# First chunk of a convolution moved from VectorE to TensorE, input weights cast once and copied, output weights scaled on GpSimd

## The chip, the cores and the metric

The kernel runs on one core of a Trainium2 chip. The time is that of the device in microseconds (us), as the median of several executions. Engines are named as the profile names them: PE is TensorE (PEld its weight loads), DVE is VectorE, ACT is ScalarE, POOL is GpSimd, SP is SyncE.

## The reference, cut to what matters

```python
# x: 8 x 4096 x 192, weight: 8 heads x 7 taps; 24 neighbouring channels share a head
w = softmax(weight)                                          # over the 7 taps
x = sum(w[head, k] * x_padded[:, s + k, :] for k in 0..6)    # causal, along the sequence
h = x.reshape(32768, 192) @ w_in                             # w_in: 192 x 2048
g = h * sigmoid(beta * h)
out = g @ w_out                                              # w_out: 2048 x 192
```

A depthwise convolution of seven taps feeds two matrix products with an activation between them.

## The kernel before

The work goes in 33 stages. A full stage is a chunk of 512 positions from each half of the batch; the first chunk is split into stages 0 and 1, of 256 positions. In stage s PE computes the hidden layer of chunk s and, interleaved with it in 16 units, the output layer of stage s-1. ACT applies the activation. DVE convolves chunks ahead of time, one tap per instruction, and also evicts PE's finished outputs from PSUM, the memory that PE's sums go to (an eviction copies them out and frees the buffer).

```python
psum_h = tile_pool("psum_h", bufs=2, PSUM)   # hidden sums, 2 banks each
psum_o = tile_pool("psum_o", bufs=2, PSUM)   # output sums "po", 2 banks each: PSUM is then full

def conv_ops(s):                             # 21 taps of DVE for stage s
    def tap(j, k):
        ...
        if k == 0:
            nc.vector.tensor_scalar_mul(dst, src, scalar)
        else:
            nc.vector.scalar_tensor_tensor(out=dst, in0=src, scalar=scalar, in1=dst, op0=ALU.mult, op1=ALU.add)
    return [lambda j=j, k=k: tap(j, k) for j in range(NG) for k in range(K)]

def output(s, u):                            # PE's output sums, then DVE's eviction of them
    ...
            if fc == NF - 1 and b == 1:
                nc.vector.tensor_copy(dst, po[:, 0, 0 : 2 * D])
                nc.vector.tensor_tensor(dst, po[:, 1, 0 : 2 * D], dst, ALU.add)
    ...

for op in conv_ops(0):
    op()
queue = deque((1, op) for op in conv_ops(1))
for c in range(0, NF, 4):
    queue.append((1, lambda c=c: prep_w_out(c, 4)))     # w_out / beta, on DVE
...
for s in range(N_ST + 1):
    if s + 2 < N_ST:
        queue.extend((s + 2, op) for op in conv_ops(s + 2))
    for u in range(NF):
        hidden(s, u)                                    # if s < N_ST
        output(s - 1, u)                                # if s > 0
        for _ in range(2 - u % 2):                      # 24 taps may be emitted per stage
            if queue:
                queue.popleft()[1]()
        ...
```

Before these stages, the first chunk is loaded as fp32, transposed on PE, and convolved by 42 taps of DVE. All later chunks come through a cast in DRAM and a transposing transfer.

## Time and profile before

The median is 722.34 us (722.22 to 722.58, three runs). Two lines of the profile's page, busy times and the chain that ended last:

```profile
PE 682.1 (95%) x11379; PEld 521.8 (73%) x11379; DVE 601.6 (84%) x965; ACT 576.9 (80%) x535; POOL 63.6 (9%) x79
...
PE 91%; DVE 6%; DMA 2%; SPq 1%; issue 0%
```

PE is busy nearly all the time, and the chain is PE's. What can be saved lies where PE is not busy. The table of stretches shows where that is. Its columns are the stretch, its length, then for each engine busy us and number of instructions, the granted clock, and two DMA columns that are not used here.

```profile
0.00:22.00 22.00, 4.99 (x19) 3.68 (x19) 5.65 (x16) 3.90 (x7) 14.57 (x25) 1.00 1.03 175
22.00:28.80 6.80, 0.79 (x4) 0.24 (x5) 6.37 (x16) 0.00 (x0) 3.14 (x4) 1.00 2.23 174
28.80:40.00 11.20, 9.23 (x94) 5.72 (x95) 10.56 (x24) 9.82 (x16) 4.09 (x5) 1.00 1.79 157
40.00:50.50 10.50, 10.43 (x214) 9.98 (x215) 10.18 (x17) 10.12 (x16) 4.55 (x5) 1.00 2.17 141
50.50:58.60 8.10, 1.24 (x18) 0.65 (x14) 7.78 (x13) 1.03 (x2) 5.20 (x6) 0.75 2.31 167
58.60:79.30 20.70, 20.67 (x280) 13.98 (x281) 19.93 (x32) 18.86 (x19) 11.56 (x14) 0.93 2.19 165
```

The first number after the length is PE. It is nearly idle to 28.8 us, works through stages 0 and 1, is nearly idle again from 50.5 to 58.6, and is full from there on. What ended the idle times from 22 to 60 us is in the table of waits (us in total, times, longest):

```profile
PE ph L256 <- DVE ct L239: 12.6, 4, 4.6
PE ph L256 <- DMA xd<-in_x_dram: 4.5, 1, 4.5
PE ph L256 <- ACT g L263: 1.2, 5, 0.4
```

PE's hidden matmuls (`ph`) wait for DVE's taps (`ct`). DVE was busy with taps nearly without a gap, and two lines of its timeline in that stretch (start, duration) show what else it did:

```profile
39.12 3.56 DVE L216 TENSOR_TENSOR w_out_s<-w_out_raw,beta_r 128x768 bf16<-128x768 f32 x4
...
49.42 0.55 DVE L296 COPY osb<-po 128x384 f32<-128x384 f32 x1
```

The second line is an eviction.

### The profile page before, as it was taken

To read this page: it belongs to the slowest core of one execution; us is meant where nothing else is said; L and a number is where in the kernel's file an instruction comes from. 1 tells how busy PE (TensorE), PEld (TensorE's weight loads), DVE (VectorE), ACT (ScalarE), POOL (GpSimd) and SP (SyncE) were. 2 spreads that over 40 slices of the span, in tenths; PEclk is the share of its full clock that TensorE was granted. 3 is DMA by queue.
4 is the path that set the end of the run, shared out by engine and by line. 5 is a ranking of instruction groups with operands and counts; after the bars stand their busy time and mean duration, and the time that the engine had idled before them with its cause. 6 is when DMAs were issued, how large, how long until landed. Compare 5 with 4: busy or idle time off the path is not lost.

```text
span 719.3 us, 24695 instructions
## 1 busy us (share of the span) xinstructions
PE 682.1 (95%) x11379; PEld 521.8 (73%) x11379; DVE 601.6 (84%) x965; ACT 576.9 (80%) x535; POOL 63.6 (9%) x79
## 2 busy tenths in 40 slices
PE   2387999999999999999999999999999999999997
PEld 2264777777777777777777777777777777777776
DVE  1999999999999889898888989888898988887223
ACT  1386888888888888888888888888888888888881
POOL 7345553000000000000000000000000000000000
PEclk9998999999999999999999999999999999999999
DMA  9999999522222231222222123222212222211012
GB/s 158 184 148 166 168 175 168 79 63 68 68 59 58 69 67 35 60 68 68 47 69 69 37 55 68 69 46 68 69 43 50 68 68 47 69 46 46 25 46 69
DMA packets 189768, 55.77 MB, mean 78 GB/s; under 512 B 153296, under 2 KB 189664, under 8 KB 189664
## 3 DMA queue, kind: packets, MB, share of 16 engines
q0 software_dynamic: 100576, 14.11, 28.9%
q1 hardware_dynamic: 89040, 40.07, 24.1%
q8 instruction: 89, 1.46, 0.8%
q14 instruction: 15, 0.12, 0.1%
q10 hardware_dynamic: 48, 0.01, 0.0%
HBM read 30.58 MB, written 37.70 MB: 95 GB/s over the span
## 4 chain that ended last, share of the span: by engine, by line
PE 91%; DVE 6%; DMA 2%; SPq 1%; issue 0%
PE po L287 46%; PE ph L256 45%; DVE ct L239 4%; DMA x_83<-in_x_dram 2%; SPq L112 1%; DVE w_out_s L216 0%; DVE ct L237 0%; PE ph L201 0%; DVE osb L297 0%; DVE osb L296 0%; DVE xt L208 0%
## 5 line engine op out<-in xcount | busy, mean ns | idle before, releaser
L263 ACT ACTIVATE g<-ph,beta 128x1024 bf16<-128x1024 f32 (+1 forms) x528 | 573.0, 1090 | 112.0 <-PE ph L256 107.9
L239 DVE SCALAR_TENSOR_TENSOR ct<-xt,cw,ct 128x512 bf16<-128x512 bf16 (+1 forms) x594 | 436.1, 734 | 17.7
L256 PE MATMUL ph<-ct,w_in_s 64*128 64x512 bf16 (+1 forms) x3168 | 429.4, 372 | 19.0 <-DVE ct L239 12.6
L287 PEld LDWEIGHTS <-g 64*128 64x128 bf16 x8192 | 369.7, 94 | 102.7 <-issue 1.2
L287 PE MATMUL po<-w_out_s,g 64*128 64x192 bf16 x8192 | 430.3, 243 | 0.1
L256 PEld LDWEIGHTS <-w_in_s 64*128 64x128 bf16 x3168 | 164.3, 94 | 75.5 <-issue 18.2
L296 DVE COPY osb<-po 128x384 f32<-128x384 f32 x128 | 71.2, 556 | 75.2 <-PE po L287 74.9
L297 DVE TENSOR_TENSOR osb<-po,osb 128x384 f32<-128x384 f32 x128 | 71.4, 558 | 4.4
L94 POOL DMA_DIRECT2D xd<-in_x_dram x62 | 56.4, 909 | 54.3 <-DMA xd<-in_x_dram 49.8
L237 DVE TENSOR_SCALAR ct<-xt,cw 128x512 bf16<-128x512 bf16 (+1 forms) x99 | 35.3, 357 | 0.0
L201 PE MATMUL ph<-ident,x_83 128*128 128x128 f32 x12 | 3.5, 432 | 8.3 <-DMA x_83<-in_x_dram 8.3
L211 ACT CAST xt<-ph 128x256 bf16<-128x256 f32 x2 | 0.7, 373 | 12.8 <-DVE xt L208 12.8
L208 DVE CAST xt<-ph 128x512 bf16<-128x512 f32 x2 | 1.4, 692 | 10.5 <-PE ph L201 10.5
L201 PEld LDWEIGHTS ph<-ident,x_83 128*128 128x128 f32 x12 | 2.2, 214 | 9.3 <-issue 9.2
L179 PE MATMUL po<-cw_92,sel 8*128 8x7 f32 x6 | 1.4, 354 | 4.5 <-DVE cw_92 L176 4.5
L156 POOL DMA_DIRECT2D w_in_s<-in_moe_w_in_dram x8 | 5.1, 647 | 0.0
L179 PEld LDWEIGHTS po<-cw_92,sel 8*128 8x128 f32 x6 | 1.3, 320 | 4.5 <-issue 4.5
L216 DVE TENSOR_TENSOR w_out_s<-w_out_raw,beta_r 128x768 bf16<-128x768 f32 x4 | 3.6, 952 | 0.0
L171 ACT ACT_TABLE_LOAD x1 | 1.3, 1283 | 2.3 <-DMA cw_92<-in_weight_dram 2.3
L169 DVE TENSOR_REDUCE nmax<-cw_92 8x1 f32<-8x7 f32 x1 | 0.1, 147 | 2.2 <-DMA cw_92<-in_weight_dram 2.2
L188 DVE COPY cw<-po 128x21 f32<-128x21 f32 x1 | 0.2, 181 | 1.7 <-PE po L186 1.7
L175 DVE RECIPROCAL rsum<-ssum 8x1 f32<-8x1 f32 x1 | 0.2, 151 | 1.6 <-ACT cw_92 L171 1.6
(19 smaller groups left out, 5.9 us busy)
## 6 DMA issues: line engine op xcount, KB each, us to landing
out_dram<-osb SPq DMA_DIRECT2D x62, 384.0 KB, 3.0
xd<-in_x_dram POOLq DMA_DIRECT2D x56, 198.0 KB, 13.9
w_in_s<-in_moe_w_in_dram POOLq DMA_DIRECT2D x8, 192.0 KB, 8.0
w_out_raw<-in_moe_w_out_dram SPq DMA_DIRECT2D x1, 1536.0 KB, 18.1
xd<-in_x_dram POOLq DMA_DIRECT2D x6, 192.0 KB, 13.8
x_83<-in_x_dram SPq DMA_DIRECT2D x8, 96.0 KB, 4.6
out_dram<-osb SPq DMA_DIRECT2D x4, 192.0 KB, 6.1
xt<-xd SPq DMA_TRANSPOSE x31, 4.9
```

The source lines that it names most:

```text
L94: nc.gpsimd.dma_start(out=xd[r0:, :, h, :], in_=x_v[p, t0:t1, h, :].rearrange("t (c d) -> t c d", c=NG),)
L112: nc.sync.dma_start(out=x0[:, b, :, h, :], in_=x_v[0, b * BLK : (b + 1) * BLK, h, :].rearrange("q (c d) -> q c d", c=NG),)
L156: nc.gpsimd.dma_start(out=w_in_s[h * DG : (h + 1) * DG, :, cols], in_=moe_w_in[:, cols].rearrange("(c d) f -> d c f", c=NG),)
L201: nc.tensor.transpose(pt[:, at // TOK, at % TOK : at % TOK + BLK], x0[:, i * half_blks + b, c, :, :].rearrange("q h d -> q (h d)"), ident,)
L216: nc.vector.tensor_tensor(w_out_s[:, c0 : c0 + n, :], w_out_raw[:, c0 : c0 + n, :], beta_r[:, c0 : c0 + n].unsqueeze(2).to_broadcast((128, ...
L237: nc.vector.tensor_scalar_mul(dst, src, scalar)
L239: nc.vector.scalar_tensor_tensor(out=dst, in0=src, scalar=scalar, in1=dst, op0=ALU.mult, op1=ALU.add)
L256: nc.tensor.matmul(ph[:, h, 0:n], w_in_s[rows, j, cols], cts[s][rows, j, 0:n], start=(j == 0), stop=(j == NG - 1),)
L263: nc.scalar.activation(gs[s][:, fc, :, 0:n], ph[:, :, 0:n], AF.Silu, scale=beta[:, fc : fc + 1])
L287: nc.tensor.matmul(po[:, r, b * D : (b + 1) * D], g[rows, fc, h, q * BLK : (q + 1) * BLK], w_out_s[rows, fc, :], start=(fc == 0), stop=(fc ...
L296: nc.vector.tensor_copy(dst, po[:, 0, 0 : 2 * D])
L297: nc.vector.tensor_tensor(dst, po[:, 1, 0 : 2 * D], dst, ALU.add)
```

## The change

The intent is to take work off DVE in the head, so that PE starts earlier. Seven diagonal matrices per channel group hold the tap weights, and PE convolves the first chunk by summing seven shifted matmuls in PSUM, with operands of type fp32r. `w_in` is cast and loaded once and copied to the other 64 partitions by DVE. `w_out` is scaled on GpSimd. The second chunk is loaded directly and transposed on PE too. Some matmuls on zeros (`fill`) are to warm up PE, that is, to keep it busy so that its clock is raised. The diff, cut to its core:

```diff
+    nc.sync.dma_start(out=beta_q, ...)         # was on the ACT queue
+    def copy_w_in(i):
+        nc.vector.tensor_copy(w_in_s[DG : 2 * DG, :, cols], w_in_s[0:DG, :, cols])
+    def fill(n):
+        for _ in range(n):
+            nc.tensor.matmul(pc[:, 1, :], zeros[:, 0:128], zeros, start=True, stop=True)
+    fill(5)
     ...                                        # tap weights and beta into pc on PE
+    fill(3)
+    def diag_conv(s, c, pv):
+        for k in range(K):
+            nc.tensor.matmul(pv[:, c, :], diag[:, c, k, :], xt0[:, c, o + k : o + k + n],
+                             start=(k == 0), stop=(k == K - 1))
+    pv = psum_h.tile([128, 4, n0], FP32, name="ph")
+    for c in (1, 0, 2):
+        diag_conv(0, c, pv)
+        if c == 0:
+            nc.scalar.copy(ct[:, c, 0:n0], pv[:, c, :])
+        else:
+            nc.vector.tensor_copy(ct[:, c, 0:n0], pv[:, c, :])
     def prep_w_out(c0, n):
-        nc.vector.tensor_tensor(
+        nc.gpsimd.tensor_tensor(
-    for op in conv_ops(0):
-        op()
-    queue = deque((1, op) for op in conv_ops(1))
+    extra = {
+        (0, 1): first_xt,                       # transposes of the second half of chunk 0
+        (0, 3): lambda: copy_w_in(2),
+        (0, 4): first_conv,                     # its convolution on PE
+        (0, 6): lambda: copy_w_in(3),
+        (0, 8): second_xt,                      # transposes of chunk 1
+    }
+    queue = deque()
     for s in range(N_ST + 1):
         ...
+            if (s, u) in extra:
+                extra[s, u]()
-            for _ in range(2 - u % 2):
-                if queue:
+            if s > 0 or u > 8:
+                for _ in range(4 if s == 0 else 2 - u % 2):
```

## The prediction

> **What bounds the kernel now.** The table of stretches shows PE busy 20.00 of 20.00 us in nearly every 20 us stretch after 58.6 us, and PE's waits there hold one entry, 4.6 us for DVE's `ct`, which ends at 58.6. From there to the end (719.3) the kernel is PE-bound and the change leaves that work alone. Only the first 58.6 us can shrink. The chain of waits there is: issue and landing of `x_83`, eight issues at 0.6-0.7 us and the last landing at 16.4; fp32 transposes, 1.3 us; then DVE's 63 taps: 42 on 256 tokens at about 0.5 us each (18.5 to 39.1), w_out scaling 4 x 0.95 us, and 21 on 512 tokens at about 0.78 us (42.6 to 58.6, one output eviction of 1.1 us among them). Of PE's work by then, stage 0's hidden part took 28.9 to 40.0 and stage 1's 40.0 to 50.5; then PE sat idle 8.1 us.
>
> **What the change does.** It takes 42 taps (about 22 us) and the scaling (3.8 us) off DVE in the head, and halves the bytes read for `w_in_s`. It adds to DVE casts, diagonals, weight copies and evictions, to ACT seven small multiplies before the first convolution, and to PE 48 bf16 transposes (estimate 0.1 us each) and 42 fp32r matmuls of 256 columns. The Trainium skill, "FP8 and Floating Point Precision", TensorE Precision Notes, gives true fp32 four passes and describes fp32r as a truncated read; the trace's fp32 128-column matmuls run at about 0.22 us each. If fp32r needs one pass, I estimate 0.11 to 0.2 us each, 2.5 to 4 us per half; no run yet shows it.
>
> **Timeline of the changed head (estimates from those durations).** First half of x lands at about 6.5; transposes to 8.3; diagonals and xt0 to about 10; convolution and copies to about 13.5. First hidden activation at about 14 (29.3 before). Stage 0: 16 units at ACT's 0.66 us, plus about 5 us of inserted PE work: to about 29. Second chunk's transposes copied at about 26, then 21 taps, 14.9 us: `ct` of stage 2 ready at about 41. Stage 1's PE work, 10.5 us, ends at about 39.5. So stage 2 starts at about 41-42, not 58.6; DVE's conv for stage 3 then ends about when PE wants it. The gain is 17 us less some lateness I allow for: **706.0 us, 700.0 to 713.0**; faster by over 2%: 0.63, within 2%: 0.36, slower: 0.01. The 2% line is at 707.9, so this is close.
>
> **Off the path, I expect:** GpSimd's scaling, 1.7-2 us a piece ("GPSIMD Engine Reference", section 3.1, measured two-input adds 1.96 times as slow as DVE, whose piece took 0.95), done near 22 us, before its first use near 30. The casts to DRAM queue behind it; the first transposed chunk should land at 32-40, needed at 41.
>
> **What would show it.** First silu activation near 14 us; stage 2's first matmul near 41; PE without idle time after it; PE's remaining wait ahead of stage 2 on DVE's `ct`; steady-state stages unchanged at 20.7 us; DVE busy time lower by about 15-20 us.
>
> **What would make it wrong.** fp32r matmuls at four passes (0.43 us or more) add about 10 us. The scaling finishing late, through slow landing of w_out or DVE's use of shared ports, would hold back both stage 1's outputs and the casts, making `xt` for stage 3 late: PE would then wait on DVE for a DMA transpose. Slow landing of x1b (needed near 23) would hold back the 512-token taps one for one. Extra matmul time in stage 0 delays the same taps.

## The result

The changed kernel takes 719.0 us (median of four, 718.14 to 719.62), against 722.46 us before. The ratio is 0.9951 with an interval of 0.9934 to 0.9968: the same within 2%, and outside the predicted range. Here and below, a ratio is the mean time of one kernel's fast runs over that of the other's in the same rounds, so it is not quite the ratio of the quoted medians.

The page's line of busy times, then PE's waits in the whole execution (the longest four):

```profile
PE 692.2 (96%) x11465; PEld 529.2 (74%) x11465; DVE 592.2 (83%) x935; ACT 578.5 (81%) x543; POOL 67.3 (9%) x79
```

```profile
PE po L380 <- DVE osb L390: 10.7, 2, 8.3
PE ph L255 <- ACT xt_151 L268: 2.2, 1, 2.2
PE ph L255 <- DVE ct L280: 1.9, 1, 1.9
PE ph L349 <- ACT g L356: 1.3, 4, 0.5
```

The wait for taps is gone. A new one stands at the top: PE's output matmuls (`po`) wait 10.7 us in two pieces for DVE's evictions (`osb`). The stretches of the changed kernel:

```profile
30.00:44.50 14.50, 13.22 (x253) 11.97 (x254) 13.86 (x21) 14.00 (x23) 6.93 (x9) 1.00 2.00 157
44.50:54.00 9.50, 1.10 (x13) 0.40 (x8) 9.11 (x16) 1.78 (x3) 6.83 (x8) 0.82 2.44 158
```

So PE reaches stage 2 at 44.5 instead of 58.6, and then does next to nothing for 9.5 us. Its timeline there, and that of DVE:

```profile
44.23 0.54 PE L380 MATMUL po<-w_out_s,g 64*128 64x192 bf16 x8
44.56 1.18 PE L349 MATMUL ph<-ct,w_in_s 64*128 64x512 bf16 x6
54.02 0.82 PE L380 MATMUL po<-w_out_s,g 64*128 64x192 bf16 x8 [8.28 <-DVE osb L390]
```

```profile
45.21 0.35 DVE L330 TENSOR_SCALAR ct<-xt,cw 128x512 bf16<-128x512 bf16 x1
45.59 4.69 DVE L332 SCALAR_TENSOR_TENSOR ct<-xt,cw,ct 128x512 bf16<-128x512 bf16 x6
50.20 0.35 DVE L330 TENSOR_SCALAR ct<-xt,cw 128x512 bf16<-128x512 bf16 x1
50.58 2.33 DVE L332 SCALAR_TENSOR_TENSOR ct<-xt,cw,ct 128x512 bf16<-128x512 bf16 x3
52.82 0.55 DVE L389 COPY osb<-po 128x384 f32<-128x384 f32 x1
53.41 0.56 DVE L390 TENSOR_TENSOR osb<-po,osb 128x384 f32<-128x384 f32 x1
...
61.47 0.55 DVE L389 COPY osb<-po 128x384 f32<-128x384 f32 x1
```

The taps of stage 2 end at 45.2. From 45.21 on DVE runs eleven taps of stage 3, which PE needs only a stage later, and then, at 52.82, the first eviction of stage 0's outputs. The matmuls of those outputs had ended near 39. There are two `po` buffers; stage 0's outputs fill both, so the first output matmul of stage 1's chunk (54.02) has to wait for the first eviction. The second is evicted at 61.47, though its sums were complete near 44.8. The Trainium skill, "TensorE: Matmul & The Clock Gate" (Part 1, architectural detail), says that ACT and DVE are strict FIFO; the trace agrees, as an eviction that was free to run from 39 us started 13.8 us later, behind taps.

How much of the lead was lost where can be read from the first activation of each stage (start in us, from ACT's timeline; the lead is the difference):

| stage | before | changed | lead |
|---|---|---|---|
| 0 | 29.31 | 19.79 | 9.5 |
| 1 | 40.51 | 34.10 | 6.4 |
| 2 | 59.34 | 45.84 | 13.5 |
| 3 | 76.60 | 72.05 | 4.6 |
| 4 | 97.52 | 95.58 | 1.9 |
| 30 | 641.44 | 639.50 | 1.9 |

A lead of 13.5 us is there at stage 2. Stage 2 then takes 26.2 us instead of 17.3 (8.3 of the 8.9 us more is the first wait), and stage 3 takes 23.5 instead of 20.9 (2.4 of the 2.6 is the second). After that every stage takes 20.92 us in both kernels. The profiled executions end 1.8 us apart; over all timed runs the medians differ by 3.5.

### The profile page after: what moved, and what is told of

The parts are those of the page before. It is cut to its first block, busy times and chain, and to the rows that moved or that the text cites. A ratio compares the mean times of both kernels' runs of the same rounds, so it can differ in the third digit from the quotient of the medians.

```text
span 717.5 us, 24845 instructions
## 1 busy us (share of the span) xinstructions
PE 692.2 (96%) x11465; PEld 529.2 (74%) x11465; DVE 592.2 (83%) x935; ACT 578.5 (81%) x543; POOL 67.3 (9%) x79
## 3 DMA queue, kind: packets, MB, share of 16 engines
q1 hardware_dynamic: 85392, 39.67, 23.5%
## 4 chain that ended last, share of the span: by engine, by line
PE 90%; DVE 7%; ACT 1%; DMA 1%; issue 0%; SPq 0%; DVEq 0%
PE po L380 45%; PE ph L349 43%; DVE ct L332 5%; DMA beta_q<-in_moe_beta_dram 1%; PE ph L255 1%; DVE ct L330 0%; DVE osb L390 0%; PE po L255 0%; DVE osb L389 0%; ACT diag L266 0%; ACT g L356 0%; DVE w_in_s L151 0%; PE po L240 0%; PE po L201 0%; DVE diag L228 0%
## 5 line engine op out<-in xcount | busy, mean ns | idle before, releaser
L380 PEld LDWEIGHTS <-g 64*128 64x128 bf16 x8192 | 369.9, 94 | 113.8 <-issue 12.5
L380 PE MATMUL po<-w_out_s,g 64*128 64x192 bf16 x8192 | 430.9, 243 | 11.0 <-DVE osb L390 10.7
L332 DVE SCALAR_TENSOR_TENSOR ct<-xt,cw,ct 128x512 bf16<-128x512 bf16 x558 | 418.6, 750 | 16.6
L330 DVE TENSOR_SCALAR ct<-xt,cw 128x512 bf16<-128x512 bf16 x93 | 32.9, 354 | 0.0
L255 PE MATMUL ph<-xt_151,diag 128*128 128x256 f32 x21 | 5.6, 439 | 4.6 <-ACT xt_151 L268 2.2
L255 PEld LDWEIGHTS ph<-xt_151,diag 128*128 128x128 f32 x21 | 4.7, 326 | 5.4 <-ACT xt_151 L268 2.4
L306 POOL TENSOR_TENSOR w_out_s<-w_out_raw,beta_r 128x768 bf16<-128x768 f32 x4 | 5.9, 1468 | 5.3 <-DMA w_out_raw<-in_moe_w_out_dram 3.8
L201 PE MATMUL po<-zeros 128*128 128x512 bf16 x8 | 3.8, 627 | 1.3 <-DVE warm L134 1.3
L266 ACT ACTIVATE diag<-ident,cw 128x128 fp32r<-128x128 f32 x7 | 2.2, 389 | 3.4 <-DVE beta L220 3.4
L151 DVE COPY w_in_s<-w_in_s 64x1536 bf16<-64x1536 bf16 x4 | 4.5, 1135 | 0.1
L255 PEld LDWEIGHTS po<-xt_151,diag 128*128 128x128 f32 x21 | 2.5, 189 | 0.3 <-issue 0.3
L255 PE MATMUL po<-xt_151,diag 128*128 128x256 f32 x21 | 2.7, 285 | 0.0
```

The costliest lines, as they stand in the source:

```text
L151: nc.vector.tensor_copy(w_in_s[DG : 2 * DG, :, cols], w_in_s[0:DG, :, cols])
L201: nc.tensor.matmul(pc[:, 1, :], zeros[:, 0:128], zeros, start=True, stop=True)
L255: nc.tensor.matmul(pv[:, c, :], diag[:, c, k, :], xt0[:, c, o + k : o + k + n], start=(k == 0), stop=(k == K - 1),)
L306: nc.gpsimd.tensor_tensor(w_out_s[:, c0 : c0 + n, :], w_out_raw[:, c0 : c0 + n, :], beta_r[:, c0 : c0 + n].unsqueeze(2).to_broadcast((128, ...
L380: nc.tensor.matmul(po[:, r, b * D : (b + 1) * D], g[rows, fc, h, q * BLK : (q + 1) * BLK], w_out_s[rows, fc, :], start=(fc == 0), stop=(fc ...
```

## The experiments

Theory "order": the evictions wait behind taps that nobody needs yet, only because of the order of emission. Rival "work": DVE has too much to do before stage 4 in any order (it is busy without a real gap from 30 to past 90 us), so the wait would only move. A third question is whether the late start of the head (first activation at 19.8 us, not 14) matters. All edits are to the changed kernel unless said otherwise, and all runs gave correct results. The kernel before took 722.0 to 722.6 us in these rounds.

### The order alone

```diff
-            if s > 0 or u > 8:
+            if s > 1 or (s == 0 and u > 8):      # no taps emitted during stage 1
```

> Only the emission order on DVE changes: during stage 1 no taps are emitted, so the two evictions of stage 0's outputs follow the 21 taps of stage 2 directly, ahead of the taps of stage 3. No instruction is added or taken away. Theory order (the evictions stand behind taps that nobody needs yet, and with two output buffers PE stops): PE's waits on the eviction, 10.7 us in the changed kernel, shrink to about 3 us in all (mostly before stage 3, on its taps), stage 3 starts near 65 instead of 72, and the time falls by 6 to 10 us, to 709 to 713. Theory work (DVE simply has more work before stage 4 than fits, in whatever order): the wait only moves from the evictions to the taps, and the time stays within 2 us of 719.

Measured: 707.52 us (706.74 to 708.64), ratio to before 0.9797, interval 0.9781 to 0.9814 (so the side of the 2% line is unclear, but the 11.5 us below the changed kernel are far outside the spread). PE's waits on taps and evictions, and DVE's timeline where the evictions now stand:

```profile
PE ph L349 <- DVE ct L332: 0.8, 1, 0.8
...
PE po L380 <- DVE osb L390: 0.7, 1, 0.7
```

```profile
40.81 4.69 DVE L332 SCALAR_TENSOR_TENSOR ct<-xt,cw,ct 128x512 bf16<-128x512 bf16 x6
45.42 0.55 DVE L389 COPY osb<-po 128x384 f32<-128x384 f32 x1
46.00 0.56 DVE L390 TENSOR_TENSOR osb<-po,osb 128x384 f32<-128x384 f32 x1
46.48 0.55 DVE L389 COPY osb<-po 128x384 f32<-128x384 f32 x1
47.06 0.56 DVE L390 TENSOR_TENSOR osb<-po,osb 128x384 f32<-128x384 f32 x1
47.54 0.35 DVE L330 TENSOR_SCALAR ct<-xt,cw 128x512 bf16<-128x512 bf16 x1
```

The same instructions, with the two evictions directly after stage 2's taps. The 10.7 us of waits become 1.5. Stage 4's first activation comes at 84.97 instead of 95.58. Theory order holds; theory work falls. The gain was even somewhat over my range. The waits account for 9.2 us of it. Most of the rest is PE's clock, which neither theory had: after the idle time the changed kernel ran at half clock until 57.4 us. In the two lines of the table of stretches, first of the changed kernel and then of this one, the third number from the end is the granted clock. It is lower by 0.09 over 18 us, which gives an estimate of 1.6 us.

```profile
54.00:72.00 18.00, 17.98 (x230) 11.88 (x231) 17.29 (x27) 15.31 (x15) 10.25 (x12) 0.91 2.18 166
```

```profile
54.00:72.00 18.00, 17.18 (x265) 12.09 (x262) 17.37 (x28) 15.95 (x16) 9.02 (x10) 1.00 2.13 159
```

### Half as many taps held back

```diff
-                for _ in range(4 if s == 0 else 2 - u % 2):
+                for _ in range(4 if s == 0 else u % 2 if s == 1 else 2 - u % 2):
```

> Between the changed kernel and the one that holds the taps back: during stage 1 one tap of stage 3 is emitted in every second unit (8 in all, 3 of them ahead of the first eviction, where the changed kernel has 11). Theory order, with the durations of the trace put through a small model of the two queues: the first wait on the eviction falls from 8.3 us to about 2.5, stage 3 starts near 64, a further wait of about 2.5 us comes in stage 3, and the time lands between the two, 709 to 714. Theory work: no difference to the changed kernel.

Measured: 711.42 us, between the two, with PE waiting 3.3 us for evictions in two pieces, 1.7 the longest. The time follows how many taps stand ahead of the evictions: 11, 3 and 0 taps ahead of the first one give 719.0, 711.4 and 707.5 us.

### Scaling of the output weights back on DVE

```diff
-        nc.gpsimd.tensor_tensor(w_out_s[...], w_out_raw[...], beta_r..., ALU.mult)
+        nc.vector.tensor_tensor(w_out_s[...], w_out_raw[...], beta_r..., ALU.mult)   # called after second_xt
```

> Undoes one part: the output weights are scaled on DVE again, right before the 512-token taps, instead of on GpSimd. Theory DVE chain (after 30 us every microsecond of DVE work in front of stage 4 is a microsecond of time): four pieces of 0.95 us, so 3 to 4 us slower, 722 to 723, no better than the kernel before. Rival (GpSimd's slower scaling holds something back): the casts start at about 8 us instead of 19, and the time stays or falls.

Measured: 721.85 us, 2.9 us slower than the changed kernel, though the DRAM casts now start at 7.9 us instead of 19.0. The four pieces of 0.95 us on DVE cost 2.9 us here, so giving the scaling to GpSimd was worth about 3 us. That DVE time before stage 4 always costs its own length is not shown: the experiment on the input weights below does not confirm it.

### Beta's load back on the ACT queue

```diff
-    nc.sync.dma_start(out=beta_q, ...)
+    nc.scalar.dma_start(out=beta_q, ...)
```

> Only beta's load goes back to the ACT queue, ahead of nothing. In the changed kernel it is issued third on the SP queue and lands at 6.0 us, while the first half of x is already cast at 5.0; cw and so the diagonals wait for it. Theory: the whole head, and the start of the 512-token taps on DVE (30.2 us) with it, comes 1 to 2.5 us earlier, and because DVE runs without a gap from there to 79 us, the time falls by as much: 716.5 to 718. Rival (the start of the head has slack): the first activation comes earlier and the time does not change.

Measured: 718.82 us, no different from the changed kernel (its runs span 718.14 to 719.62). The first activation came 1.0 us earlier (18.78), as foreseen, but the lead was lost within stage 0. PE's timeline of the second half's convolution, first in the changed kernel, then in this one:

```profile
23.37 2.74 PE L255 MATMUL po<-xt_151,diag 128*128 128x256 f32 x21
```

```profile
23.11 3.97 PE L255 MATMUL po<-xt,diag 128*128 128x256 f32 x21
```

The same 21 matmuls took 1.2 us longer. Neither theory had that (the held-back order's kernel had it too, 3.61 us); the last experiment returns to it.

### Input weights loaded twice

```diff
+        for h in range(2):                       # both partition halves by casting transfers
             nc.gpsimd.dma_start(out=w_in_s[h * DG : (h + 1) * DG, :, cols], ...)
-        nc.vector.tensor_copy(w_in_s[DG : 2 * DG, :, cols], w_in_s[0:DG, :, cols])
```

> Undoes one part: the input weights are loaded by two casting transfers into both partition halves, as before, and the four DVE copies (4.5 us in all) go. Of these only the first (1.8 us) and in part the others stand in front of the first taps. Theory DVE chain: 1 to 3 us faster if the transfers keep up; if the doubled weight traffic makes the second chunk of x land after about 28 us, the gain is lost or turns into a loss. I expect 716 to 720.

Measured: 718.52 us, within the spread of the changed kernel. In the profiled execution the taps of stage 2 start 2.2 us earlier (28.0), but over the timed runs no gain is clear. Loading once and copying neither helps nor hurts by more than about 1 us here.

### The convolution on DVE again, in the good order

To the first experiment's kernel, the core of the change is undone: `conv_ops(0)` and `conv_ops(1)` take the place of the two diagonal convolutions, and `xt0` is bf16 again.

```diff
-    for c in (1, 0, 2):
-        diag_conv(0, c, pv)
-        ...
+    for op in conv_ops(0):
+        op()
     def first_conv():
-        ...
+        for op in conv_ops(1):
+            op()
```

> The held-back order, with the core of the change undone: the first chunk is convolved by DVE's 42 taps again instead of by diagonal matmuls; loads, weight copies, GpSimd's scaling and the order stay. The taps are 22 us; the diagonals, the casts to fp32r and the evictions that go are about 5 us of DVE. So the 512-token taps start about 15 to 17 us later (near 46), and the time is 720 to 724, no better than the kernel before: the move to TensorE carries the whole gain, once the order lets it. Rival (the gain of the held-back order comes from the order alone or from the other parts of the change): the time stays below 713.

Measured: 719.22 us, so 11.7 us slower than the same order with TensorE's convolution. The time is just under the range that I expected, and the taps of stage 2 start at 41.0 and not near 46: in the held-back order's kernel DVE had waited 4.4 and 4.0 us for PE's convolutions, which I had not counted, and here it does not. The rival is out. PE's longest waits are again those of the kernel before:

```profile
PE ph L311 <- DVE ct L253: 17.7, 4, 8.6
```

So TensorE's convolution and the order together give 707.5 us; with the first alone the time is 719.0, with the second alone (and the rest of the change) 719.2. Each is worth about 11.5 us once the other is in place.

### The start of the head

Three kernels on top of the held-back order. The first brings beta early, gives the warm-up its own PSUM tile (the copy of the tap weights had a wait of 2.9 us that ended with the warm-up matmuls, which write the same tile), and adds warm-up before the first convolution:

```diff
-    nc.sync.dma_start(out=beta_q, ...)
+    nc.scalar.dma_start(out=beta_q, ...)
+    pf = psum_h.tile([128, 2, TOK], FP32, name="ph")
-            nc.tensor.matmul(pc[:, 1, :], zeros...
+            nc.tensor.matmul(pf[:, 0, :], zeros...
-    fill(3)
+    fill(1)
     pt = transposes(x0b, 0, HB)
+    fill(5)
```

> On top of the held-back order: beta's load on the ACT queue, the warm-up matmuls in a tile of their own (so that the copy of the tap weights no longer waits for them) and five more of them after the transposes, so that PE is busy up to the first convolution. If the first convolution runs at half speed because PE idles before it (0.25 us a matmul there, 0.13 in the second half), it now takes 0.13 us. Expected: first activation near 15 instead of 18.4, the 512-token taps start 2 to 4 us earlier, time 703.5 to 706. If the head has slack somewhere later, the time stays at 707.5.

Measured: 706.06 us (703.27 to 707.03), first activation at 16.55 instead of 18.39. The median is 1.5 us lower, but its runs scatter and overlap with the kernel it builds on. The added warm-up missed its aim in the profiled execution: the matmuls of the first half's convolution still start 0.21 us apart, and not at the expected 0.13.

The second gives each convolution result a tile of its own:

```diff
-    pv = psum_h.tile([128, 4, n0], FP32, name="ph")
     for c in (1, 0, 2):
+        pool, name = (psum_o, "po") if c == 0 else (psum_h, "ph")
+        pv = pool.tile([128, 4, n0], FP32, name=name)
         diag_conv(0, c, pv)
```

> On top of the held-back order: each of the three convolution results gets its own PSUM tile, so that the second and third convolution need not wait for the copies of the one before (0.8 + 0.5 us of waits in that kernel, 1.9 + 0.5 in the changed one), and each copy no longer waits for later matmuls. Expected: first activation 1 to 2 us earlier, time 705.5 to 707.5.

Measured: 704.61 us, first activation at 16.46. In the one shared tile each convolution had waited for the copy of the result before it, although it writes other columns; the waits are gone. They were 0.8 and 0.5 us, and the gain is 2.9, more than I expected. In this trace PE's clock was also released at 14.8 us instead of 24.6 (see the last experiment), so the tiles alone are not shown to give it.

The third has both:

> Held-back order, early beta, warm-up in its own tile and separate convolution tiles together. If the start of the 512-token taps on DVE sets the time, as the order theory says of what is left, the gains add: taps start near 26, time 702 to 705. If stage 1 on PE or the second chunk's landing takes over, less.

Measured: 702.14 us (700.88 to 702.7), first activation at 13.73, taps of stage 2 from 23.05 us. With the order mended, the start of the head does set the time, nearly one for one: the lead of 4.7 us at stage 0 is 5.4 us at the end.

### Second chunk two units earlier

```diff
-        (0, 6): lambda: copy_w_in(3),
-        (0, 8): second_xt,
+        (0, 6): second_xt,
+        (0, 8): lambda: copy_w_in(3),
```

> The fastest version so far (702.1), with the second chunk's transposes moved two units earlier in stage 0, in exchange with the last weight copy. DVE's 512-token taps then start about 1.2 us earlier (near 21.9) if the second chunk has landed by then, and the time falls by 0.5 to 1.5 us, to 700.6 to 701.6; if the chunk lands after 20 us, PE waits for it and nothing is gained.

Measured: 700.85 us (700.77 to 701.67), ratio to before 0.9703, interval 0.9688 to 0.9717. This is the fastest version, 3.0% under the kernel before and about 18 us under the changed one. PE's waits that are left on DVE's taps and evictions:

```profile
PE ph L353 <- DVE ct L336: 1.5, 2, 0.8
...
PE po L384 <- DVE osb L394: 0.7, 1, 0.7
```

### Without the warm-up before the convolution

From the fastest version, the five warm-up matmuls between the transposes and the convolution are taken out.

```diff
     pt = transposes(x0b, 0, HB)
-    fill(5)
```

> The fastest version (700.85), without the five warm-up matmuls between the transposes and the first convolution, so PE idles about 1.7 us there. Theory (the first convolution runs at half speed after idle time): the matmuls of the second and third channel group, 0.21 and 0.14 us apart with the warm-up, go back to about 0.25 to 0.27 us, the first activation comes 1 to 2 us later and the time rises by 1 to 2 us, to about 702 to 703. Rival (the first half's matmuls are slow for another reason, such as their operands being fresh): spacing and time do not change.

Measured: 702.0 us (701.8 to 702.76), 1.15 us slower. PE's timeline of the three convolutions of the first half, with the warm-up and without (start, duration, seven matmuls each):

```profile
8.71 2.06 PE L257 MATMUL ph<-xt,diag 128*128 128x256 f32 x7
10.57 1.30 PE L257 MATMUL po<-xt,diag 128*128 128x256 f32 x7
11.70 0.98 PE L257 MATMUL ph<-xt,diag 128*128 128x256 f32 x7
```

```profile
8.69 1.86 PE L257 MATMUL ph<-xt,diag 128*128 128x256 f32 x7 [1.67 <-ACT xt L270]
10.35 1.70 PE L257 MATMUL po<-xt,diag 128*128 128x256 f32 x7
11.85 1.16 PE L257 MATMUL ph<-xt,diag 128*128 128x256 f32 x7
```

The slow spacing lasts through the first group in both and ends earlier with the warm-up; the whole block ends 0.3 us earlier (12.68 against 13.01). The Trainium skill, "TensorE: Matmul & The Clock Gate" (Part 1), says that an idle PE is gated to half its clock and released after about 3.4 us of activity. The traces agree with the factor: from start to start, the convolution's matmuls are 0.21 us apart when slow and 0.12 us when fast, and the hidden layer's bf16 matmuls in the changed kernel go from 0.21 us apart (before 23 us) to 0.11 (from 26 us on), so this is no matter of fp32r or of fresh operands.

The packed traces also hold the changes of the granted clock. The first record in each, a full clock, starts where the spacing changes: at 11.2 us in the fastest version, 12.2 without the warm-up, 23.2 in the changed kernel, and 24.6 in the held-back order and 25.8 in the beta experiment, both in the middle of the second half's convolution, which is why that took longer. So the slow matmuls are those before the clock's release; that PE had half its clock until then is inferred, as nothing is recorded before. The time of 3.4 us fits after the later idle times (the half clock ended 3.3 us after PE resumed in the changed kernel, 2.8 us in the kernel before), but in the head, where PE has short idle times from its first matmul (2.5 us) on, the release came much later, and in the first head kernel, with the same five warm-up matmuls, it came only at 21.8 us. What sets the moment of the release is not shown, and one profiled execution of each kernel does not show that the warm-up brought it forward.

Nor is the 1.15 us shown to be the worth of the warm-up. Stage 1's first activation comes at 27.71 instead of 26.46; 0.3 us of that is the convolution's, and about 0.9 is lost at the second chunk's transposes. There PE waits for the chunk to land, which it does not in the fastest version:

```profile
PE po L242 <- DMA x1b<-in_x_dram: 0.7, 1, 0.7
```

Its second chunk landed 12.4 to 13.5 us after its issue, against 11.1 to 12.2 in the fastest version. But it landed at 12.5 to 13.6 in the third head kernel, which has the warm-up, so this difference need not come from the edit. The two kernels were also timed in different rounds.

## Why the prediction was wrong

- "Only the first 58.6 us can shrink" and steady stages unchanged: right. Stages took 20.92 us in both kernels.
- "First hidden activation at about 14": wrong, it came at 19.8. The mis-sized terms: xt0 was done at 11.2 and the last diagonals at 12.2 instead of about 10 (x was early, but beta landed at 6.0 and the copy of the tap weights waited for warm-up matmuls); and the convolution took from 10.8 to 18.8 us instead of about 3.5 us, because each group of seven fp32r matmuls in the first half took 1.86 us (PE's clock was not yet released, see the last experiment) and because PE waited twice for copies out of a shared PSUM tile, which I had not counted. The head experiments brought the activation to 13.5.
- "2.5 to 4 us per half" for fp32r: right for the second half (2.74 us), wrong for the first (three groups of 1.86 us and waits). The estimate came from 0.22 us for an fp32 matmul of 128 columns, but those matmuls (6.0 to 17.4 us of the kernel before) also ran ahead of the release of the clock, which that trace records at 34.1 us. Like for like, before the release, fp32 transposes of 128 columns and fp32r matmuls of 256 columns both start 0.21 us apart, a factor of two per column. The Trainium skill's "FP8 and Floating Point Precision" (TensorE Precision Notes) gives true fp32 four passes; a factor of four is not what these numbers show.
- "Stage 2 starts at about 41-42": near, 44.6. The lead at stage 2 was 13.5 to 14 us.
- "DVE's conv for stage 3 then ends about when PE wants it", and with it "PE without idle time after it": this is the step that failed. I added up DVE's work and compared its end with PE's need of the taps, but did not place the evictions in DVE's queue. The compiled order, which was at hand, had eleven taps of stage 3 ahead of the first eviction. Before the change such an order cost nothing, because PE was waiting for stage 2's taps until 58.6 anyway, and the first eviction (49.42) was done by then. Once PE ran ahead, it stopped on its two output buffers: 10.7 us. With the order mended the time was 707.5, inside the predicted range. That does not make the rest of the sum right: stage 2 still began about 3 us later than foreseen, which the range allowed for.
- "DVE busy time lower by about 15-20 us": wrong, it fell by 9.4 us (601.6 to 592.2). The casts, diagonals, copies and evictions that came to DVE took more than was allowed for.
- The scaling on GpSimd: in time (done at 19.1 us) and worth 2.9 us. The casts and transposes behind it were in time too: no wait for them is in PE's list. It was not free for DVE: a copy of 64x1536 bf16 that started while a GpSimd multiply ran took 1.84 us and ended about 0.5 us after it; the same copy took 0.68 us where it started first. These are single instances, without an experiment on them alone.

What stays open: what sets the moment at which PE's clock is released (11.2 to 25.8 us in the runs named here), whether the warm-up gains anything, and whether an order better than the tried ones exists.

## What to carry to other kernels

When a change lets one engine run ahead, look at what stands in the in-order queue of the engine that frees its buffers: work that is early there can be harmless until the engine that needs the buffers gets ahead, and then it can cost nearly its full length (here 7.6 us of taps stood behind a wait of 8.3 us). Compare not only sums of work but the position of each release among the work around it. A small move in emission order can be worth as much as the change itself, and each may show nearly nothing without the other.

## What the Trainium skill lacked or had wrong

- "GPSIMD Engine Reference", section 3.1: it gives two-input adds 1.96 times DVE's time. The operation here is not the same one: the scaling (a multiply of two fp32 inputs, one of them broadcast, bf16 out, 768 elements per partition) took 1.47 us on GpSimd and 0.95 us on DVE, 1.54 times.
- "TensorE: Matmul & The Clock Gate": no rate is given for fp32r. Here matmuls with 128x128 weights and 256 columns start 0.12 us apart at full clock and 0.21 us apart before its release.
- "TensorE: Matmul & The Clock Gate", Part 1: it does not say that a profile's clock records can begin only with the release. Here the changed kernel's trace has none before 23.2 us, and the table of stretches counts such time as full clock: it reads 1.00 for 10.8 to 18.8 us, where the convolution's matmuls started 0.21 us apart, and 1.00 for 23.3 to 26.2 us, where they started 0.12 us apart.
